# Two groups of heads change places, stack loads are spread over key tiles, and the late output sums move to VectorE

## The chip, the cores and the metric

The kernel runs on one core of one Trainium2 chip. The core has a matrix engine (TensorE, PE in the profile, with its weight loads as PEld), a vector engine (VectorE, DVE), an activation engine (ScalarE, ACT), a general engine (GpSimd, POOL) and a queue engine (SyncE, SP). Transfers (DMAs) are issued from the instruction queues of SP, GpSimd and ScalarE, and 16 DMA engines carry them out. Each engine works through its own instructions in order and waits for others by semaphores.

The metric is the time of the device in microseconds (us) for one execution; of several executions the median counts, less is better.

## The reference: what is computed

One transformer layer over 2048 tokens of width 576, in float32: layer norm, attention with 32 heads of 18 columns each, a residual sum, layer norm again, and a gated feed-forward network of width 4608 with its own residual sum.

```python
qkv = (x @ wqkv).reshape(B, S, 3, H, Dh)          # H = 32 heads, Dh = 18
scores = einsum("bhqd,bhkd->bhqk", q, k) * Dh ** -0.5
o = einsum("bhqk,bhkd->bhqd", softmax(scores), v)
h = x + o.transpose(0, 2, 1, 3).reshape(B, S, D) @ wo   # x was normalised before wqkv
h2 = h + (gelu(hn @ w_gate) * (hn @ w_up)) @ w_down     # hn = layernorm(h)
```

Column f of `o` (0 to 575), and so row f of `wo`, belongs to head f // 18.

## The kernel before, in words

**Numbers in two halves.** Most products are made of float16 numbers, each float32 number cut into a high and a low part, with three products for one. The high and low parts of q and k go to two tensors in device memory, `qk_hi` and `qk_lo` (L343), and come back as *stacks*: for each head 54 rows that hold high, high, low of q against high, low, high of k.

**Groups, blocks, key tiles.** The 32 heads form `NG` = 8 groups of four, and the 2048 queries form `NB` = 4 blocks of 512. The attention loop (L1352) runs over n = 0 to 31 with group g = n // 4 and query block qc = n % 4, and in each n over `kt` = 0 to 15, the key tiles of 128 keys. For one key tile `score` (L702) makes the scores of four heads on TensorE and their exponentials on ScalarE (L723, L725), and `weigh` (L729) multiplies them with V and with a column of ones, whose result is the sum for the softmax. In the same loop `maxima` (L809) makes the row maxima for a query block that comes one and a half n later: scores on TensorE (L645), maxima on VectorE (L659, L657). What an engine does is in the order in which the program writes it out (the kernel switches automatic ordering off for all engines); pieces of side work are written as generators, and `take(it)` puts the next piece at that place of the order.

**Stacks.** There are two sets of stacks. `load_stacks(g)` (L583) writes one set with 24 transfers of 18 rows by 2048 (72 KB each): 12 for the first pair of heads, issued from SP, and 12 for the second, issued from GpSimd. `load_ends(g)` (L612) issues 8 smaller transfers from SP; `key_steps(g)` (L621) makes differences of keys from them on GpSimd, which `maxima` uses. The loop calls both loads for the next group at kt = 10 of the group's first block (L1390; at kt = 2 of the second block in group 0), `key_steps` at kt = 10 and 13 of its second block. For group 0 all this stands ahead of the loop (L1323 to L1325).

**Output of one block.** `out_block(n)` (L744) runs in three pieces during n + 1. First, at kt = 1 (0 from late in n = 30 on), ScalarE and VectorE copy the sums out of PSUM, and a transfer fetches the softmax denominators (L752). At kt = 3 the reciprocals are made (GpSimd up to n = 27, VectorE after that), sent to device memory (L767) and broadcast back to all rows by four transfers from SP (L770). At kt = 9 (6 for the blocks n = 29 and 30) the output is multiplied with them, and cut into a high and a low part (L773 to L779): on GpSimd for n up to 29, on VectorE for n = 30 and 31. Then the rows go by transfers into `XT`, the left operand of the product with `wo` (L783 to L799). `XT` holds the 576 columns of `o` in four chunks of 128 and a last one of 64. A transfer of 18 rows that lies in one of the first four chunks carries both parts (L795); rows of the last chunk need one transfer for the high and one for the low part (L799). Each head has two halves of 256 queries. So the rows of heads 28 to 31 (columns 504 to 575, of which 512 to 575 are in the last chunk) need 18 transfers, those of other groups mostly 8. The queues take turns: SP and GpSimd, for n = 30 ScalarE too, for n = 31 SP, GpSimd, SP, GpSimd, ScalarE.

**Product with wo, and the late part of the loop.** From kt = 9 of n = 30 on the maxima are done, and the loop takes half a tile of the product with `wo` at each key tile instead (step `L` of `LATE`, L1347): `wo_pairs` for the tokens of query blocks 0 and 1 (the tiles 0, 4, 1, 5 and so on), then `wo_block(2)`. One half is 14 matmuls (L325) that read `XT` in the order of its chunks, and one operation of VectorE that adds the residual (L875). Rows that are ready go on to the second layer norm and to the first sums of the feed-forward network (`rows0`, on VectorE, GpSimd and SP's transposes). Beside it GpSimd cuts weights of the feed-forward network from n = 28 on (`split_early`, and the sums of `split_matrix`, L1077). `wo` itself is scaled and cut by `prepare_wo` (L835) during n = 2, with a few VectorE operations on its scales at both ends (L838, L845, L846).

**Ahead of the loop.** Weights of q, k and v come in by `load_w` and `load_chunks` from SP, the v weights in three transfers into `wf[2]` (L498), whose norm ScalarE takes at L180. `v_rows` (L387) puts V's columns into the groups' places by their number.

## Time and profile before

| | |
|---|---|
| time before, median of 3 runs | 2592.74 us (2591.53 to 2593.41) |
| the profiled execution | 2588.55 us, of which 2586.8 us from the first to the last instruction (span) |
| granted clock of TensorE, mean | 0.997 |
| TensorE busy | 2532.3 us (98%) |
| VectorE busy | 1991.4 us (77%) |
| ScalarE busy | 1664.1 us (64%) |
| GpSimd busy | 908.3 us (35%) |
| transfers | 120.99 MB, mean 47 GB/s |

The span has three stretches: q, k and v with the first maxima (to about 205 us), the attention (about 205 to 1376 us, one n in some 35 us until late in n = 30), and the feed-forward network (to the end). In the profile's lines a group of instructions is named by line, engine and operation, with the tiles it writes and reads (`X<-nat` is a transfer of output rows into `XT`, `rc` the reciprocals, `mx` the maxima, `WK` the exponentials, `A` and `W` the two sets of stacks). "Idle before" is the time in which the engine stood still just before an instruction, with what ended it; "issue" there means that the engine waited for nothing that the profile shows.

### The profile page before, as it was taken

What the parts mean: (1) busy time and instruction counts of PE and PEld (TensorE: products, weight loads), DVE (VectorE), ACT (ScalarE), POOL (GpSimd) and SP (SyncE); (2) the same over time, 40 slices, a digit from 0 to 9 for tenths busy, and PEclk for the clock granted to TensorE, in tenths of its full rate; (3) what the DMA queues carried; (4) which work ended last, traced back from release to release, by engine and by line L of the source; (5) the groups of instructions that cost most, each with busy time, mean ns of one, the idle gap of its engine ahead of it and who ended that gap; (6) DMA issues with size and microseconds to landing.
All of it is one profiled execution on the core that took longest, in us unless ns stands there. A gap on an engine that the chain in (4) does not pass through costs nothing.

```text
span 2586.8 us, 96735 instructions
## 1 busy us (share of the span) xinstructions
PE 2532.3 (98%) x41245; PEld 1440.3 (56%) x41245; DVE 1991.4 (77%) x3887; ACT 1664.1 (64%) x2967; POOL 908.3 (35%) x1290
## 2 busy tenths in 40 slices
PE   8999999999999999999989999999999999999999
PEld 4645555555555555555555555555555555555555
DVE  8479999999999999999856674757575756565653
ACT  7438999999999999999845433424242434333332
POOL 4301634432434333346946332323132323232221
PEclk9999999999999999999999999999999999999999
DMA  8621010110101010101234410101010101010110
GB/s 223 159 70 53 19 46 22 26 41 18 47 19 49 21 46 21 44 22 35 57 76 93 85 51 12 53 12 37 28 34 30 35 30 35 30 34 30 34 56 37
DMA packets 177086, 120.99 MB, mean 47 GB/s; under 512 B 93854, under 2 KB 153433, under 8 KB 176653
## 3 DMA queue, kind: packets, MB, share of 16 engines
q1 hardware_dynamic: 162987, 96.18, 14.0%
q0 software_dynamic: 13312, 18.54, 2.8%
q8 instruction: 322, 5.28, 0.9%
q14 instruction: 111, 0.91, 0.1%
q10 hardware_dynamic: 354, 0.08, 0.0%
HBM read 80.05 MB, written 15.01 MB: 37 GB/s over the span
## 4 chain that ended last, share of the span: by engine, by line
PE 74%; DVE 14%; ACT 6%; issue 3%; POOL 2%; DMA 1%; SPq 0%; ACTq 0%; DVEq 0%; POOLq 0%
PE more L1209 14%; PE bank L1209 14%; PE bank L325 10%; DVE mx L659 9%; PE more L325 8%; PE bank L645 6%; PE bank L737 5%; ACT WK L725 4%; PE quad L737 4%; PE quad L325 3%; DVE nat L657 3%; PE pair L714 2%; PE bank L714 2%; PE quad L645 1%; PE pair L325 1%
## 5 line engine op out<-in xcount | busy, mean ns | idle before, releaser
L659 DVE TENSOR_REDUCE mx<-bank 128x1 f32<-128x512 f32 x1064 | 707.4, 683 | 23.4 <-PE bank L645 21.5
L737 PE MATMUL bank<-WK,V 64*32 64x256 f32 x8192 | 636.6, 379 | 8.2 <-ACT nat L748 8.0
L737 PE MATMUL quad<-WK,V 64*32 64x256 f32 x8192 | 639.4, 380 | 0.4 <-issue 0.2
L725 ACT ACTIVATE WK<-bank 128x512 f32<-128x512 f32 x780 | 543.3, 700 | 1.8 <-PE bank L714 1.6
L1209 PEld LDWEIGHTS <-W 128*128 128x128 f16 x2394 | 233.9, 98 | 278.9 <-issue 0.4
L325 PEld LDWEIGHTS <-WK 128*128 128x128 f16 x3456 | 338.0, 98 | 88.6 <-POOL WK L1223 0.3
L725 ACT ACTIVATE WK<-quad 128x512 f32<-128x512 f32 x488 | 345.3, 708 | 0.5 <-PE quad L714 0.3
L659 DVE TENSOR_REDUCE mx<-pair 128x1 f32<-128x512 f32 x488 | 336.8, 690 | 3.9 <-PE pair L645 0.4
L723 ACT ACTIVATE WK<-pair 128x1024 f32<-128x1024 f32 x268 | 293.7, 1096 | 47.1 <-PE pair L714 37.1
L737 PEld LDWEIGHTS quad<-WK,V 64*32 64x32 f32 x8192 | 236.4, 106 | 26.2 <-issue 0.9
L645 PEld LDWEIGHTS <-W 54*32 54x32 f16 x4096 | 140.8, 89 | 179.3 <-issue 116.8
L737 PEld LDWEIGHTS bank<-WK,V 64*32 64x32 f32 x8192 | 216.5, 105 | 34.1 <-ACT nat L748 17.4
L325 PE MATMUL more<-W,WK 128*128 128x288 f16 x1728 | 235.4, 286 | 0.0
L325 PE MATMUL bank<-W,WK 128*128 128x288 f16 x1728 | 235.3, 286 | 0.0
L759 POOL TENSOR_TENSOR rp<-rc,minus_one 128x4 f32<-128x4 f32 x112 | 111.4, 1009 | 340.7 <-DMA rc<-nat 340.7
L645 PEld LDWEIGHTS <-A 54*32 54x32 f16 x4096 | 132.2, 89 | 175.7 <-issue 118.5
L1209 PE MATMUL more<-X,W 128*128 128x512 f16 x792 | 223.9, 379 | 0.0
L645 PE MATMUL bank<-W 54*32 54x512 f16 x2048 | 203.5, 383 | 7.4 <-DVE mx L659 0.9
L645 PE MATMUL bank<-A 54*32 54x512 f16 x2220 | 202.8, 383 | 6.8 <-DVE mx L659 0.4
L1077 POOL TENSOR_TENSOR A<-A 128x384 f32<-128x384 f32 x136 | 137.3, 1030 | 199.4 <-DMA A<-in_B_w_up_dram 99.8
L1209 PE MATMUL more<-V,W 128*128 128x512 f16 x720 | 202.5, 379 | 0.0
L1223 POOL TENSOR_TENSOR WK<-tmp,WK 128x512 f16<-128x512 f32 x73 | 88.7, 1214 | 306.7 <-ACT WK L1220 306.5
(361 smaller groups left out, 5053.5 us busy)
## 6 DMA issues: line engine op xcount, KB each, us to landing
A<-in_B_w_down_dram SPq DMA_DIRECT2D x8, 1152.0 KB
nat<-rc SPq DMA_DIRECT2D x128, 64.0 KB
A<-in_B_w_gate_dram SPq DMA_DIRECT2D x64, 128.0 KB
A<-in_B_w_up_dram SPq DMA_DIRECT2D x64, 128.0 KB
qk_hi<-tmp SPq DMA_DIRECT2D x36, 128.0 KB
qk_lo<-tmp SPq DMA_DIRECT2D x36, 128.0 KB
out_dram<-nat SPq DMA_DIRECT2D x16, 288.0 KB
nat<-in_A_x_dram SPq DMA_DIRECT2D x3, 1152.0 KB
```

The costliest lines, as they stand in the source:

```text
L325: nc.tensor.matmul(dst, a, b, start=(i == 0), stop=(i == len(pairs) - 1))
L645: mm = [nc.tensor.matmul(pm[c : c + CT, :TB], Q[r, q0 + c : q0 + c + CT], keys, start=True, stop=True) for c in range(0, P, CT)]
L657: nc.vector.tensor_tensor_reduce(row, pm[:, :TB], row, 1.0, LOWEST, ALU.add, ALU.max, dst)
L659: red = nc.vector.tensor_reduce(dst, pm[:, :TB], axis=AX.X, op=ALU.max)
L714: mm.append(nc.tensor.matmul(pS[c : c + CT, :TB], K[r, k0 : k0 + CT], Q[r, qc * TB : (qc + 1) * TB], start=True, stop=True))
L723: act = nc.scalar.activation(pe, pair, AF.Exp, scale=ex_reg)
L725: act = nc.scalar.activation(pe[:, heads[0] % 2], bank_at(bank)[:, :TB], AF.Exp, scale=ex_reg)
L737: nc.tensor.matmul(acc[CT * c : CT * c + CT, :QH], Vg[n // NB][ks, v : v + CT], pes[(2 * kt + q) % NPE][ks, j, qh * QH : (qh + 1) * QH], s ...
L759: nc.gpsimd.tensor_tensor(rc[:, c : c + 4], den[:, c : c + 4], minus_one.to_broadcast([P, 4]), op=ALU.pow)
L1077: op(W8[:, d], W8[:, a], W8[:, b])
L1209: nc.tensor.matmul(bank, w, x_, start=start and i == 0, stop=i == len(mm) - 1, skip_group_check=not start)
L1223: nc.gpsimd.tensor_sub(hl[:, 2 * i + j], v, hh[:, 2 * i + j])
```

## The change

The work stays the same; its order, its places and its queues differ.

1. `ORDER` lets the last two groups change places: group 6 of the loop handles heads 28 to 31, group 7 heads 24 to 27. The columns of V's weights are loaded so that these groups find theirs at the usual place: nine transfers of 432, 72 and 72 columns instead of three of 576.
2. `load_stacks` becomes a generator that yields after each pair of transfers (one from SP, one from GpSimd), and `load_group` puts one transfer of `load_ends` behind each of the first eight pairs. From the same place in the loop as before, one such step is taken at each key tile. For group 0 all steps are run at once.
3. In `out_block` VectorE makes the products and cuts of n = 29 too. The rows go out from SP and GpSimd in turn, for n = 29 from SP, SP, GpSimd; ScalarE issues none of them any more.
4. The third piece of `out_block` for n = 29 is taken at kt = 8 of n = 30 instead of 6, that of n = 30 at kt = 5 of n = 31 instead of 6.
5. The scales of `wo` are made ahead of the loop by `scale_wo`; `prepare_wo` only cuts.

```diff
--- before.py
+++ after.py
@@ -347,6 +347,7 @@
 
 
 
+    ORDER = [g for g in range(NG) if g != NG - 2] + [NG - 2]
     G4 = 4 * VC
     VGAP = 768
     VH = NG // 2
@@ -495,7 +496,10 @@
     load_chunks(wf[1], wqkv[:, D:QK], nc.sync, range(2, NK + 1))
     load_x(1)
     qk_tiles(0, 0)
-    load_w(wf[2], wqkv[:, QK:], nc.sync)
+    G72 = 4 * DH
+    for a, b, n_ in ((0, 0, (NG - 2) * G72), ((NG - 2) * G72, (NG - 1) * G72, G72),
+                     ((NG - 1) * G72, (NG - 2) * G72, G72)):
+        load_w(wf[2][:, :, a : a + n_], wqkv[:, QK + b : QK + b + n_], nc.sync)
     take(n1, 4)
     qk_tiles(0, 1)
     take(n1, 1)
@@ -582,18 +586,15 @@
 
     def load_stacks(g):
         st = sets[g % 2]
-        for pr in range(2):
-            eng = nc.sync if pr == 0 else nc.gpsimd
-            Q, K = st[pr]
-            for j in range(2):
-                h = 4 * g + 2 * pr + j
-                o = 64 * j
-                kr = slice(D + h * DH, D + (h + 1) * DH)
-                qr = slice(h * DH, (h + 1) * DH)
-                for i, (qs, ks) in enumerate(((qk_hi, qk_hi), (qk_hi, qk_lo), (qk_lo, qk_hi))):
-                    rows = slice(o + i * DH, o + (i + 1) * DH)
-                    eng.dma_start(Q[rows], qs[qr])
-                    eng.dma_start(K[rows], ks[kr])
+        for j in range(2):
+            o = 64 * j
+            for i, (qs, ks) in enumerate(((qk_hi, qk_hi), (qk_hi, qk_lo), (qk_lo, qk_hi))):
+                rows = slice(o + i * DH, o + (i + 1) * DH)
+                for m, src in ((0, qs), (1, ks)):
+                    for pr, eng in enumerate((nc.sync, nc.gpsimd)):
+                        f = m * D + (4 * ORDER[g] + 2 * pr + j) * DH
+                        eng.dma_start(st[pr][m][rows], src[f : f + DH])
+                    yield
 
     nat1 = nat.rearrange("p t d -> p (t d)")
     HB = NB // 2
@@ -611,12 +612,20 @@
 
     def load_ends(g):
 
-        kr = slice(D + 4 * g * DH, D + (4 * g + 1) * DH)
+        kr = slice(D + 4 * ORDER[g] * DH, D + (4 * ORDER[g] + 1) * DH)
         for e, src in zip(ends, (qk_hi, qk_lo)):
             for s in range(DQ):
                 nc.sync.dma_start(
                     e[s * DH : (s + 1) * DH],
                     src[kr].rearrange("r (k s i) -> r k s i", k=NB, s=DQ)[:, :, s])
+                yield
+
+    def load_group(g):
+
+        it = load_ends(g)
+        for _ in load_stacks(g):
+            take(it)
+            yield
 
     def key_steps(g):
 
@@ -769,7 +778,7 @@
         for c in range(4):
             nc.sync.dma_start(rcb[32 * c : 32 * c + 32], rd_rows[c : c + 1].to_broadcast([32, TB]))
         yield
-        if n < NS - 2:
+        if n < NS - 3:
             nc.gpsimd.tensor_mul(oT, oT, rcb)
             nc.gpsimd.tensor_copy(ohl[:, 0], oT)
             nc.gpsimd.tensor_sub(ohl[:, 1], oT, ohl[:, 0])
@@ -777,11 +786,10 @@
             nc.vector.tensor_mul(oT, oT, rcb)
             (nc.scalar.copy if n == NS - 1 else nc.vector.tensor_copy)(ohl[:, 0], oT)
             nc.vector.tensor_sub(ohl[:, 1], oT, ohl[:, 0])
-        engs = ring([nc.sync, nc.gpsimd] + ([nc.scalar] if n == NS - 2 else
-                                            [nc.sync, nc.gpsimd, nc.scalar] if n == NS - 1 else []))
+        engs = ring([nc.sync, nc.gpsimd] if n != NS - 3 else [nc.sync, nc.sync, nc.gpsimd])
         quads_of = ohl.rearrange("p s (i c) -> i p s c", i=2)
         for hh in range(4):
-            f, end = (4 * g + hh) * DH, (4 * g + hh + 1) * DH
+            f, end = (4 * ORDER[g] + hh) * DH, (4 * ORDER[g] + hh + 1) * DH
             r = 0
             while f < end:
                 c, p = divmod(f, P)
@@ -834,14 +842,20 @@
 
     def prepare_wo():
 
-        e_o = e_wo[0]
-        s_o = pow2(e_o, -1, 268, "s_wo")
+        s_o = scales_o[0]
         for c in range(NK + 1):
             nc.gpsimd.tensor_scalar_mul(of[:, c], of[:, c], s_o)
             yield
             nc.gpsimd.tensor_copy(oh[:, c], of[:, c])
             nc.gpsimd.tensor_sub(ol[:, c], of[:, c], oh[:, c])
             yield
+
+    scales_o = []
+
+    def scale_wo():
+
+        e_o = e_wo[0]
+        scales_o.append(pow2(e_o, -1, 268, "s_wo"))
         nc.vector.tensor_add(e_o, e_o, e_keep)
         nc.vector.tensor_copy(u_o, pow2(e_o, 1, -151, "u_wo"))
 
@@ -1320,8 +1334,7 @@
     qk_tiles(3, 0)
     init_set(sets[0])
     qk_tiles(3, 4, 5)
-    load_stacks(0)
-    load_ends(0)
+    run(load_group(0))
     run(key_steps(0))
     load_w(of, wo, nc.gpsimd)
     sums = chain(norm_wo(), raw_norms())
@@ -1338,6 +1351,7 @@
             take(sums)
         if i == 5 * AHEAD // 4 - 6:
             nc.scalar.activation(root, eps, AF.Exp)
+            scale_wo()
     run(sums)
     m_ring = ring([singles[2], quads[1]])
     accs = (singles[3], quads[2])
@@ -1349,6 +1363,7 @@
     rows_at = {4 * (i + 1) + k: c for i in range(TPB) for k, c in ((1, 2), (3, 3), (4, 3))}
     rows = rows0()
     in_order.enter_context(tc.manual_schedule(engines={EngineType.SP}))
+    loads = iter(())
     for n in range(NS):
         g, qc = divmod(n, NB)
         late = n > NS - NB
@@ -1372,7 +1387,7 @@
                 else:
                     take(side)
             halves += [(n, kt, accs, q) for q in range(2)]
-            if n and kt in (2 if n == NS - 1 else 3, 6 if n > NS - 3 else 9):
+            if n and kt in (2 if n == NS - 1 else 3, {NS - 1: 5, NS - 2: 8}.get(n, 9)):
                 take(ob)
             if n == NS - NB + 1 and 4 <= kt < 9:
                 nc.sync.dma_start(nat[:, kt - 4], xv[:, kt - 4])
@@ -1388,8 +1403,8 @@
                 run(fill)
                 init_set(sets[1])
             if g + 1 < NG and (qc, kt) == ((1, 2) if g == 0 else (0, 10)):
-                load_stacks(g + 1)
-                load_ends(g + 1)
+                loads = load_group(g + 1)
+            take(loads)
             if g + 1 < NG and qc == 1 and kt == 10:
                 steps_made = key_steps(g + 1)
                 take(steps_made)
```

## The prediction, made before the changed kernel was run

> **What bounds the kernel now.** I read the page first, then the table of 65 us windows, then the timelines of single engines where a window falls short. TensorE is the engine to look at: its line on the page, then the windows (per row: length, busy us of PE, PEld, DVE, ACT and POOL, granted clock, DMA share, GB/s).
>
> ```profile
> PE 2532.3 (98%) x41245; PEld 1440.3 (56%) x41245; DVE 1991.4 (77%) x3887; ACT 1664.1 (64%) x2967; POOL 908.3 (35%) x1290
> ```
>
> ```profile
> 325.00:390.00 65.00, 62.78 (x1867) 35.58 (x1864) 63.32 (x120) 63.83 (x120) 23.01 (x41) 1.00 0.16 44
> ...
> 520.00:585.00 65.00, 62.42 (x1856) 34.70 (x1851) 63.43 (x120) 63.61 (x119) 24.84 (x41) 1.00 0.15 36
> 585.00:650.00 65.00, 63.69 (x1908) 35.94 (x1893) 64.34 (x124) 65.00 (x123) 18.16 (x32) 1.00 0.07 17
> 650.00:715.00 65.00, 63.15 (x1904) 35.46 (x1888) 64.31 (x122) 64.61 (x121) 28.63 (x48) 1.00 0.18 46
> ...
> 910.00:975.00 65.00, 63.40 (x1884) 35.28 (x1873) 64.03 (x123) 64.48 (x122) 28.02 (x49) 1.00 0.17 47
> ...
> 1495.00:1560.00 65.00, 65.00 (x388) 37.97 (x387) 48.34 (x100) 27.42 (x39) 20.19 (x19) 1.00 0.14 41
> ```
>
> In the attention ScalarE has no gap at all (65.00 of 65 in the row at 585, as in most), so there every microsecond in which ScalarE idles is lost. After 1376 TensorE is full (65.00 in the last row): what is saved earlier is kept to the end. The big losses lie between, in the last two query blocks, where TensorE sets the pace. TensorE's timeline there (start, length, and in brackets the idle time before and who ended it):
>
> ```profile
> 1287.48 1.28 PE L325 MATMUL bank<-W,X 128*128 128x288 f16 x9
> 1290.54 0.54 PE L325 MATMUL bank<-W,X 128*128 128x288 f16 x3 [1.78 <-DMA X<-nat]
> 1296.00 0.64 PE L325 MATMUL bank<-W,X 128*128 128x288 f16 x2 [4.92 <-DMA X<-nat]
> ...
> 1299.16 1.89 PE L325 MATMUL quad<-W,X 128*128 128x288 f16 x14
> ...
> 1333.02 1.89 PE L325 MATMUL quad<-W,X 128*128 128x288 f16 x14
> ...
> 1336.30 1.89 PE L325 MATMUL bank<-W,X 128*128 128x288 f16 x14
> ...
> 1344.08 0.63 PE L714 MATMUL pair<-W 56*32 56x512 f16 x8 [5.30 <-ACT WK L723]
> ...
> 1346.46 3.54 PE L325 MATMUL quad<-W,X 128*128 128x288 f16 x14
> ...
> 1351.46 0.79 PE L325 MATMUL bank<-W,X 128*128 128x288 f16 x5
> ```
>
> One key tile with its half product of wo takes 1336.30 - 1333.02 = 3.28 us. The first stall stretches one of them to 1299.16 - 1287.48 = 11.68, a loss of 8.40 (6.70 idle, 1.70 slow). The second: 1351.46 - 1336.30 = 15.16 for two, a loss of 8.60 (5.30 idle, 3.30 slow). The slow part is the clock, in windows of the same columns:
>
> ```profile
> 1292.12:1298.95 6.83, 2.95 (x50) 1.19 (x50) 0.52 (x1) 0.73 (x1) 1.44 (x3) 0.50 0.39 110
> ...
> 1343.32:1350.15 6.83, 6.07 (x54) 2.82 (x61) 0.11 (x1) 3.58 (x6) 1.86 (x3) 0.50 0.03 6
> ```
>
> Half clock follows both stalls, so removing a stall removes its slow part too. The Trainium skill ("TensorE: Matmul & The Clock Gate", "Why this matters for your kernels") says that one idle window of some 3 us halves the clock; the trace agrees (5.30 us idle, then 0.50). By its penalty (throttled time times a half) the two windows would cost 6.8 us where the spacing shows 5.0, since TensorE still idles in part of them; the sum would be 1.8 better.
>
> **First stall: the sums of the block before (n = 29).** GpSimd, SP and VectorE:
>
> ```profile
> 1281.38 4.00 POOL L1077 TENSOR_TENSOR A<-A 128x384 f32<-128x384 f32 x4
> 1285.34 1.28 POOL L773 TENSOR_TENSOR nat<-nat 128x512 f32<-128x512 f32 x1
> ```
>
> ```profile
> 1272.41 2.96 SPq L770 DMA_DIRECT2D nat<-rc  x4
> ...
> 1289.36 6.03 SPq L799 DMA_DIRECT2D X<-nat  x8
> ```
>
> ```profile
> 1279.08 0.68 DVE L657 CUSTOM_DVE_ANT_0 nat<-quad,nat 128x512 f32<-128x512 f32 x1
> ```
>
> The broadcast reciprocals are issued by 1275.4, but GpSimd, in order, first cuts weights until 1285.3, sums until 1288.5, and then SP needs to 1295.4 for its half of 18 row transfers (eight of its nine in the row). TensorE gets on at 1296.0. After the change VectorE does the sums at kt = 8, right behind its last maximum, which ends at 1279.8. Their price on VectorE is shown one block later, with ScalarE's share of that block's rows:
>
> ```profile
> 1336.43 0.69 DVE L777 TENSOR_TENSOR nat<-nat 128x512 f32<-128x512 f32 x1
> ...
> 1337.62 0.69 DVE L779 TENSOR_TENSOR nat<-nat 128x512 f16<-128x512 f32 x1
> ```
>
> ```profile
> 1337.62 5.28 ACTq L799 DMA_DIRECT2D X<-nat  x6
> 1343.01 1.02 ACT L723 ACTIVATE WK<-pair 128x1024 f32<-128x1024 f32 x1 [8.46 <-DMA X<-nat]
> ```
>
> 1338.31 - 1336.43 = 1.9, so the sums are ready at 1281.7 instead of 1288.5. The last group now holds heads 24 to 27, output rows 432 to 503, all in one chunk of 128: 8 transfers of 18 rows (L795) instead of 18. Six go to SP, two to GpSimd:
>
> ```profile
> L795 POOL DMA_DIRECT2D X<-nat x128: 520/593/788, 262.7 to 1393.0; - x128
> L795 SPq DMA_DIRECT2D X<-nat x128: 645/786/1381, 263.5 to 1389.3; - x128
> ```
>
> ```profile
> X<-nat POOLq DMA_DIRECT2D x100, 18.0 KB, 1.8
> ```
>
> The sixth of SP starts at 1281.7 + 5 x 0.79 = 1285.6 and lands some 1.8 later (GpSimd's row; SP's landing is not shown): 1287.4. GpSimd's two start when the four additions of L1077 end, 1285.4 at the latest, and land by 1285.4 + 0.6 + 1.8 = 1287.8. Chunk 3 is wanted by the tenth of the 14 products, at 1288.76 (1287.48 + 1.28). That is 1 us of margin: I take the whole 8.40, and keep 0 to 8.40 for the range. Behind the sums on VectorE waits only L875 of kt = 9, whose product is not ready before 1282.8; no maxima are left. If the broadcast landed late VectorE would wait with that L875 behind it, and TensorE two halves later; but it has 1279.8 - 1275.4 = 4.4 us to land.
>
> **Second stall: the rows of n = 30.** ScalarE waits for VectorE's sums, issues six transfers, and only then computes the exponentials (8.46 idle). The change leaves this block to SP and GpSimd, 4 transfers each, 4 x 0.79 = 3.2 us, so ScalarE waits for nothing: 8.60. What is late next is the rows themselves, wanted by the product of block 2 at kt = 9, two key tiles (6.6 us) after 1336.30, so at 1342.9. Issued one key tile earlier than now (kt = 5), at about 1335 behind SP's transposes, they land by 1335 + 3.2 + 1.8 = 1340. Covered. The last block (n = 31) loses ScalarE's transfers too; TensorE has no gap there, so 0.
>
> **Stacks, one pair of transfers a key tile.** The loads of the next group start at kt = 10 of its first block, now 24 stack and 8 end transfers at once. Shortly after, TensorE waits for nothing that the profile shows:
>
> ```profile
> 380.54 0.39 PE L645 MATMUL quad<-W 54*32 54x512 f16 x2 [1.01 <-issue]
> ```
>
> ScalarE's missing time in the windows of such loads is 1.17 + 1.39 + 0.39 + 0.52 = 3.47 us (rows 325, 520, 650, 910), against 0.00 in the row at 585, which has none. I read it as code that comes late behind the burst. Spread, a pair (144 KB) and an end transfer go out every 2.2 us. Bounds: 0 if the cause is another, 3.5 if all goes; I take 3.3. The queues they pass: SP's wait for the reciprocals at kt = 1 to 3 delays the last pairs by a few us, and they are first read at kt = 8 of the third block, over 40 us on. On GpSimd each costs 0.5 us, as now.
>
> **The prelude pays.** SP's transfers, TensorE's first maxima, the read of V's weights, and the load's windows:
>
> ```profile
> 22.42 0.59 SPq L285 DMA_DIRECT2D WK<-in_A_wqkv_dram  x1
> ...
> 99.80 3.63 SPq L617 DMA_DIRECT2D nat<-qk_lo  x4
> ```
>
> ```profile
> 30.25 0.67 ACT L180 ACTIVATE A<-WK 128x576 f16<-128x576 f32 x1
> ```
>
> ```profile
> 102.61 0.77 PE L645 MATMUL bank<-A 54*32 54x512 f16 x16
> ```
>
> ```profile
> 88.00:100.50 12.50, 12.50 (x104) 9.98 (x103) 0.00 (x0) 8.38 (x30) 4.91 (x11) 1.00 0.60 154
> 100.50:105.00 4.50, 4.50 (x48) 3.04 (x46) 1.95 (x4) 2.55 (x10) 0.70 (x2) 1.00 0.20 40
> ```
>
> V's columns come in 9 transfers instead of 3: 6 x 0.59 = 3.5 us more on SP, ending at 23.0 + 3.5 = 26.5, before ScalarE reads them at 30.25. Bounds 0 and 3.5; I take 0.5. In the first load the end transfers now stand among the stacks, so the last stack leaves SP last, by 103.4 (where the ends are now), and the second maximum wants it at 102.7. The transfers themselves end with 0.20 x 4.5 = 0.9 us of work after 100.5, so about 101.4 if nothing idles; bounds 0 and 8.5; I take 0.5.
>
> **Small parts.** The scale of wo moves ahead of the loop. Its four late operations sit on a full VectorE now:
>
> ```profile
> 308.16 0.72 DVE L845 CUSTOM_DVE_ANT_0 e_wo<-e_wo,e_keep 128x2 uint16<-128x2 uint16 x1
> ...
> 309.37 0.69 DVE L659 TENSOR_REDUCE mx<-bank 128x1 f32<-128x512 f32 x1
> ```
>
> From 308.16 to 309.37 is 1.2 us; ahead of the loop VectorE has room. Bounds 0 and 1.2; I take 0.5. Heads 28 to 31 take the 18 row transfers in blocks 24 to 27: 5 more of 0.5 us on GpSimd, busy 28 of 65 there (row 910); 0 while that idle time covers it, 2.5 a block if not.
>
> **Sum.** 8.4 + 8.6 + 3.3 + 0.5 - 0.5 - 0.5 = 19.8 us. The profiled execution took 2588.55 (span 2586.8), 4.2 below the median 2592.74; so 2568.8 for it, and 2592.74 - 19.8 = 2572.9 for the median.
>
> **Rivals.** *The first stall stays in part*: the rows land after 1288.76, because GpSimd's two come late or VectorE waits. For it: 1 us of margin. Against: all inputs are there 4 us early. Up to 8.4 back; with half, 2577. *The gaps after the stack loads stay*: their cause is not the burst. For it: the profile names none, and the loads differ (1.39 against 0.39; three of the seven show next to nothing). 2572.9 + 3.3 = 2576.2. The Trainium skill ("Runtime: NRT & Kernel Launch", "Instruction fetch mechanics") speaks for this one: code is fetched in blocks while the one before executes, "mostly hidden"; by that 2576.2. The stall of 1.01 "issue" speaks against it. *Slower: every pair costs what a burst costs now.* A burst costs 3.47 / 7 = 0.5 us; seven groups with 12 pairs each would make 42 us, so 2572.9 + 3.3 + 42 = 2618. It decides from (2592.74 - 2576.2) / 84 = 0.2 us a pair. Against: the four broadcasts of every block go out as closely and leave ScalarE at 65.00:
>
> ```profile
> 397.51 1.71 SPq L770 DMA_DIRECT2D nat<-rc  x4
> ```
>
> **Chances.** Forecast 0.72, first stall in part 0.12, gaps stay 0.11, slower 0.05. No change can be told within 0.2% (5.2 us): faster 0.94, same 0.02, slower 0.04. Range: at the low end the whole of every gain without the prelude's cost (8.4 + 8.6 + 3.5 + 1.2 = 21.7, so 2571), less the runs' spread and gaps not listed, 2565; at the high end the first stall's whole 8.4 back, 2581.3, with the spread 2583.
>
> **What would show it.** No idle time of TensorE over 1 us at L325 or L714 in the last two blocks, clock 1.00 there, key tiles 3.28 us apart; sums of n = 29 on VectorE about 1.9 us right behind the last maximum; no transfer in ScalarE's queue there; ScalarE at 65.00 in the windows with loads; no new gap of TensorE before its first maxima. A TensorE gap before `X` in the last blocks, or ScalarE's gaps at group changes unchanged, would prove the matching part wrong.

## The result, and the profile after

| | before | after |
|---|---|---|
| median (6 runs each) | 2589.65 us (2584.45 to 2593.41) | 2570.51 us (2569.81 to 2573.94) |
| ratio, 95% interval | | 0.993 (0.9916 to 0.9944) |
| profiled execution, span | 2588.55, 2586.8 us | 2570.03, 2568.2 us |
| TensorE's granted clock, mean | 0.997 | 1.0 |

The prediction used the first three of the six runs of before (2592.74). The changed kernel is 19.1 us faster by the medians, 18.5 us by the profiled executions; 19.8 was predicted. Lines of the changed kernel stand some ten further down: L654 and L668 are the maxima (L645, L659 before), L732 the exponentials (L723), L746 and L757 the product with V and the copy of its sums (L737, L748), L786 to L788 VectorE's sums (L777 to L779), L803 the row transfers (L795), L889 the residual (L875), L1091 the cut of weights (L1077).

TensorE's line on the page of the changed kernel, against 2532.3 us before; TensorE does the same matmuls:

```profile
PE 2526.9 (98%) x41245; PEld 1439.5 (56%) x41245; DVE 1992.3 (78%) x3890; ACT 1664.1 (65%) x2967; POOL 908.0 (35%) x1290
```

The waits of TensorE in the changed kernel from 1262 to 1359 us (the last two query blocks), all of them (us in total, times, longest), and its timeline there:

```profile
PE bank L746 <- ACT nat L757: 0.3, 1, 0.3
```

```profile
1283.43 1.89 PE L325 MATMUL quad<-W,X 128*128 128x288 f16 x14
1286.71 1.89 PE L325 MATMUL bank<-W,X 128*128 128x288 f16 x14
1289.99 1.89 PE L325 MATMUL quad<-W,X 128*128 128x288 f16 x14
...
1333.70 1.89 PE L325 MATMUL bank<-W,X 128*128 128x288 f16 x14
1336.98 1.89 PE L325 MATMUL quad<-W,X 128*128 128x288 f16 x14
1340.26 1.89 PE L325 MATMUL bank<-W,X 128*128 128x288 f16 x14
```

Both stalls are gone in this execution: half a tile of the product with `wo` every 3.28 us, in both places. The sums and row transfers of n = 29 (first stall), on VectorE, SP and GpSimd:

```profile
1278.73 1.03 DVE L786 TENSOR_TENSOR nat<-nat 128x512 f32<-128x512 f32 x1
1279.85 1.06 DVE L787 CAST nat<-nat 128x512 f16<-128x512 f32 x1
1280.94 1.37 DVE L788 TENSOR_TENSOR nat<-nat 128x512 f16<-128x512 f32 x1
1282.24 0.51 DVE L889 SCALAR_TENSOR_TENSOR nat<-bank,u_o,nat 128x288 f32<-128x288 f32 x1
```

```profile
1282.34 4.92 SPq L803 DMA_DIRECT2D X<-nat  x6
```

```profile
1277.13 4.64 POOL L1091 TENSOR_TENSOR A<-A 128x384 f32<-128x384 f32 x4
1282.61 1.24 POOL L803 DMA_DIRECT2D X<-nat  x2 [0.84 <-DVE nat L788]
```

The sums stand right behind the last maximum, as predicted, but take 3.6 us (1278.73 to 1282.31), not 1.9.

The 65 us windows of the changed kernel (same columns as before):

```profile
325.00:390.00 65.00, 63.63 (x1900) 35.68 (x1892) 64.29 (x122) 64.93 (x122) 24.13 (x44) 1.00 0.16 41
520.00:585.00 65.00, 63.83 (x1912) 36.04 (x1897) 64.62 (x124) 65.00 (x122) 26.42 (x44) 1.00 0.14 36
...
650.00:715.00 65.00, 63.84 (x1912) 36.03 (x1904) 64.50 (x122) 65.00 (x122) 27.70 (x47) 1.00 0.19 49
910.00:975.00 65.00, 63.75 (x1912) 35.80 (x1890) 64.17 (x122) 64.83 (x121) 31.50 (x54) 1.00 0.19 48
```

ScalarE's missing time in these four was 3.47 us before and is 0.24 now.

To see where the gain lies, the two profiled executions are laid beside each other at points that both have: the start of the first maxima, of the first scores, of ScalarE's copy of block n's sums (L748 before, L757 after), and of the feed-forward network's first matmuls. A difference that grows between two points was lost between them:

```
start after - start before, us
first maxima   +0.66      n = 3    +1.52      n = 30      -9.16
first scores   +2.06      n = 24   -1.91      n = 31     -17.81
n = 1          +2.02      n = 29   -0.77      feed-fwd.  -17.76
n = 2          +1.58                          end        -18.54
```

So: ahead of the first scores 2.06 lost, scales of `wo` 0.44 gained (n = 1 to 2), stack loads 3.43 (n = 3 to 24), then 1.14 lost (n = 24 to 29), first stall 8.39, second 8.65, and 0.78 gained in the feed-forward network.

### The profile page after: what moved, and what is told of

Its sections match the earlier page's. It is cut to its first block, busy times and chain, and to the rows that moved or that the text cites. A ratio compares the mean times of both kernels' runs of the same rounds, so it can differ in the third digit from the quotient of the medians.

```text
span 2568.2 us, 96735 instructions
## 1 busy us (share of the span) xinstructions
PE 2526.9 (98%) x41245; PEld 1439.5 (56%) x41245; DVE 1992.3 (78%) x3890; ACT 1664.1 (65%) x2967; POOL 908.0 (35%) x1290
## 4 chain that ended last, share of the span: by engine, by line
PE 75%; DVE 13%; ACT 6%; issue 3%; DMA 1%; SPq 0%; POOL 0%; ACTq 0%; DVEq 0%; POOLq 0%
PE bank L1223 15%; PE more L1223 15%; PE bank L325 10%; DVE mx L668 9%; PE more L325 8%; PE bank L654 6%; PE bank L746 5%; ACT WK L734 5%; PE quad L746 4%; PE quad L325 3%; DVE nat L666 3%; PE pair L723 2%; PE bank L723 2%; PE quad L654 1%; PE quad L723 1%
## 5 line engine op out<-in xcount | busy, mean ns | idle before, releaser
L668 DVE TENSOR_REDUCE mx<-bank 128x1 f32<-128x512 f32 x1064 | 707.8, 683 | 25.0 <-PE bank L654 23.1
L746 PE MATMUL bank<-WK,V 64*32 64x256 f32 x8192 | 634.5, 379 | 8.0 <-ACT nat L757 7.9
L746 PE MATMUL quad<-WK,V 64*32 64x256 f32 x8192 | 637.2, 379 | 0.6 <-issue 0.4
L668 DVE TENSOR_REDUCE mx<-pair 128x1 f32<-128x512 f32 x488 | 336.8, 690 | 3.9 <-PE pair L654 0.5
L732 ACT ACTIVATE WK<-pair 128x1024 f32<-128x1024 f32 x268 | 293.5, 1095 | 28.6 <-PE pair L723 26.3
L746 PEld LDWEIGHTS quad<-WK,V 64*32 64x32 f32 x8192 | 235.7, 105 | 25.1 <-issue 0.7
L654 PEld LDWEIGHTS <-W 54*32 54x32 f16 x4096 | 140.5, 89 | 181.2 <-issue 119.1
L746 PEld LDWEIGHTS bank<-WK,V 64*32 64x32 f32 x8192 | 216.0, 105 | 32.9 <-ACT nat L757 17.4
L654 PEld LDWEIGHTS <-A 54*32 54x32 f16 x4096 | 132.4, 89 | 176.2 <-issue 118.6
L654 PE MATMUL bank<-W 54*32 54x512 f16 x2048 | 203.6, 383 | 7.1
L654 PE MATMUL bank<-A 54*32 54x512 f16 x2220 | 203.1, 383 | 7.5 <-DMA A<-qk_hi 0.9
L1091 POOL TENSOR_TENSOR A<-A 128x384 f32<-128x384 f32 x136 | 137.6, 1033 | 196.1 <-DMA A<-in_B_w_up_dram 97.7
```

What stands on the lines that cost most here:

```text
L654: mm = [nc.tensor.matmul(pm[c : c + CT, :TB], Q[r, q0 + c : q0 + c + CT], keys, start=True, stop=True) for c in range(0, P, CT)]
L668: red = nc.vector.tensor_reduce(dst, pm[:, :TB], axis=AX.X, op=ALU.max)
L732: act = nc.scalar.activation(pe, pair, AF.Exp, scale=ex_reg)
L746: nc.tensor.matmul(acc[CT * c : CT * c + CT, :QH], Vg[n // NB][ks, v : v + CT], pes[(2 * kt + q) % NPE][ks, j, qh * QH : (qh + 1) * QH], s ...
L1091: op(W8[:, d], W8[:, a], W8[:, b])
```

## Experiments

Single profiled executions are compared at the same points. Each figure is the change against the kernel before over that stretch; a minus is a gain. "After, again" is a second profiled execution of the changed kernel; the last three kernels come in the section on the first scores:

```
kernel (us, profiled execution)   first     n=3 to   n=24 to  n=29 to  n=30 to
                                  scores    n=24     n=29     n=30     n=31
after            2570.03          +2.06    -3.43    +1.14    -8.39    -8.65
after, again     2569.49          +1.99    -3.42    +0.65    -8.00    -8.65
late part alone  2580.30          +0.72    +1.10    +1.15    -3.12    -7.68
no exchange      2576.48          +2.31    -4.15    +0.23    -2.98    -8.31
sums on GpSimd   2573.35          +3.49    -3.44    +0.78    -6.02    -8.61
ScalarE's queue  2576.45          +2.16    -3.44    +1.40    -8.40    -3.68
sums at kt = 9   2575.60          +6.25    -3.43    +0.69    -6.23    -8.65
all at once      2575.46          +3.40    +0.17    +1.32    -8.11    -8.65
two a key tile   2569.58          +1.98    -3.44    +0.65    -7.93    -8.65
burst at kt = 15 2590.30          +0.05    -0.19    +0.71    +0.15    +0.24
new order, gr. 0 2591.51          +1.48    -1.08    +0.99    +0.03    -1.16
old order, gr. 0 2570.21          +3.14    -3.44    +0.64    -8.40    -8.65
and V in 3, cut  2568.77          +2.16    -4.02    -0.14    -8.40    -8.65
```

### The first stall: three ways to bring it back

**The late part alone** (the kernel before, with VectorE's sums, the two queues and the key tiles of the change; places, loads and scales as before).

```diff
-        if n < NS - 2:
+        if n < NS - 3:
-        engs = ring([nc.sync, nc.gpsimd] + ([nc.scalar] if n == NS - 2 else ...
+        engs = ring([nc.sync, nc.gpsimd] if n != NS - 3 else [nc.sync, nc.sync, nc.gpsimd])
-            if n and kt in (2 if n == NS - 1 else 3, 6 if n > NS - 3 else 9):
+            if n and kt in (2 if n == NS - 1 else 3, {NS - 1: 5, NS - 2: 8}.get(n, 9)):
```

> The kernel before with the late part of the change alone: sums of n = 29 on VectorE, their rows to SP and GpSimd, the key tiles 8 and 5; no change of places, so the last heads' block still makes 18 row transfers, and the loads stay at once. Theory A (the sums' lateness and the count of transfers both made the first stall): SP's 12 of 18 leave from about 1282.3 on at 0.7 to 0.8 us each, the last lands near 1292.5 to 1293.5, some 4 us after TensorE wants it; the first stall stays at 4 to 6 us with its slow clock, the second is gone: about 11 to 13 us off the profiled execution before (2576 to 2578). Theory B (the sums' place alone decides, the change of places of the groups is not needed): both stalls gone, 17 us off (2571.5). If the second stall is still there, 0 to 4 us off.

**No exchange of places** (the changed kernel, with heads and V in the old order).

```diff
-    ORDER = [g for g in range(NG) if g != NG - 2] + [NG - 2]
+    ORDER = list(range(NG))
...
+    load_w(wf[2], wqkv[:, QK:], nc.sync)
```

> The changed kernel with the heads in their old order and V loaded in 3 transfers; all else of the change stays. Theory A: the first stall comes back in part, 4 to 6 us with its slow clock, since 18 transfers leave in the last group's block; the way to the first scores gets 0.5 to 0.8 us shorter (V in 3 transfers, of the 2.06 us that the changed kernel lost there); the 1.1 us that the changed kernel lost in blocks 24 to 29 come back if the 18 transfers that moved into blocks 24 to 27 were their cause, and stay if not. Against the changed kernel +2 to +5 us. Theory B (the change of places does nothing): 0.6 us less than the changed kernel.

**The sums of n = 29 on GpSimd** (the changed kernel; 8 transfers stay).

```diff
-        if n < NS - 3:
+        if n < NS - 2:
```

> The changed kernel with the sums of n = 29 back on GpSimd, where they stand behind its four additions that cut weights; their 8 row transfers stay. Theory A (the sums' lateness made the first stall): the sums end near 1288.5 to 1290 instead of 1282.3, the last rows land near 1295, TensorE waits 4 to 6 us and then has the half clock for a window: 6 to 8 us more than the changed kernel (2574 to 2576 for the profiled execution). Theory B (18 transfers instead of 8 made it): 8 transfers need 4 us and TensorE waits under 1 us: 0 to 1 us more.

The row transfers of SP in the kernel without the exchange and TensorE behind them; then the same two in the kernel with GpSimd's sums:

```profile
1282.08 1.51 SPq L800 DMA_DIRECT2D X<-nat  x2
1283.63 7.55 SPq L804 DMA_DIRECT2D X<-nat  x10
```

```profile
1286.40 1.65 PE L325 MATMUL bank<-W,X 128*128 128x288 f16 x12
1291.67 0.40 PE L325 MATMUL bank<-W,X 128*128 128x288 f16 x2 [3.63 <-DMA X<-nat]
```

```profile
1285.84 4.92 SPq L803 DMA_DIRECT2D X<-nat  x6
```

```profile
1287.77 1.28 PE L325 MATMUL bank<-W,X 128*128 128x288 f16 x9
1291.27 0.77 PE L325 MATMUL bank<-W,X 128*128 128x288 f16 x5 [2.22 <-DMA X<-nat]
```

In each TensorE gets on 0.5 us after SP's last issue ends (1291.18, 1290.76). Both causes are real. Of the 8.39 us, early sums alone bring 3.0 to 3.1 (two kernels; with 18 transfers TensorE still idles 3.6 us, then a half clock), 8 transfers alone bring 6.0 (2.22 us idle, full clock), both together all. Theory A holds for the kernels with 18 transfers. For GpSimd's sums its 6 to 8 us were too much: the loss is 2.4, since the half clock did not come. The exchange of places carries the larger part. How the eight transfers are divided between the queues (six to SP, two to GpSimd) was not varied by itself.

The totals of the two kernels with 18 transfers miss what was expected. The late part alone is 8.25 us ahead of the kernel before instead of 11 to 13: at the second stall TensorE still waits 0.8 us (0.5 for rows, 0.3 for VectorE), and 0.72, 1.10 and 1.15 are lost elsewhere (table). The kernel without the exchange is 6.5 us behind the changed one instead of 2 to 5, of which 1.5 go to a window of half clock after the first scores (last section); its first scores come no earlier (+2.31), though V has 3 transfers there.

**Sums one key tile later** (kt = 9) measures the margin.

```diff
-            if n and kt in (2 if n == NS - 1 else 3, {NS - 1: 5, NS - 2: 8}.get(n, 9)):
+            if n and kt in (2 if n == NS - 1 else 3, {NS - 1: 5}.get(n, 9)):
```

> The changed kernel with the sums of n = 29 and their rows one key tile later, at 9 instead of 8 (3.28 us, and behind one more operation of VectorE). Theory A (the margin is 0.7 to 1 us): TensorE waits for the rows 2 to 3 us, without a window of half clock or with a short one: 2 to 4 us more than the changed kernel. Theory B (the rows are wanted later than I read it, the margin is over 3 us): 0.

```profile
1288.19 4.92 SPq L803 DMA_DIRECT2D X<-nat  x6
```

```profile
1290.44 1.28 PE L325 MATMUL bank<-W,X 128*128 128x288 f16 x9
1293.72 0.77 PE L325 MATMUL bank<-W,X 128*128 128x288 f16 x5 [2.00 <-DMA X<-nat]
```

At kt = 9 GpSimd's additions are over before the sums begin, and each is as short as the prediction had it:

```profile
1281.30 4.00 POOL L1091 TENSOR_TENSOR A<-A 128x384 f32<-128x384 f32 x4
```

```profile
1286.24 0.68 DVE L786 TENSOR_TENSOR nat<-nat 128x512 f32<-128x512 f32 x1
1287.01 0.43 DVE L787 CAST nat<-nat 128x512 f16<-128x512 f32 x1
1287.48 0.69 DVE L788 TENSOR_TENSOR nat<-nat 128x512 f16<-128x512 f32 x1
```

So the same sums take 1.9 us apart from these additions and 3.6 beside them, and the additions 4.00 and 4.64.

Lost: 2.16 us, as theory A said (most of what its total has beside that lies ahead of the first scores, below). TensorE got on 0.6 us after SP's last issue ended (1293.11). In the changed kernel SP's last issue ends at 1287.26 and chunk 3 is wanted at 1286.71 + 1.28 = 1287.99, so by 0.5 to 0.6 us its margin is 0.1 to 0.2 us. It just fits, and not in each execution: in the second one of the changed kernel VectorE's first product took 1.50 us instead of 1.03, and TensorE waited for the rows (0.31 us with two steps a key tile):

```profile
1286.16 1.28 PE L325 MATMUL bank<-W,X 128*128 128x288 f16 x9
1287.68 0.77 PE L325 MATMUL bank<-W,X 128*128 128x288 f16 x5 [0.24 <-DMA X<-nat]
```

### The second stall: ScalarE's queue

```diff
-        engs = ring([nc.sync, nc.gpsimd] if n != NS - 3 else [nc.sync, nc.sync, nc.gpsimd])
+        engs = ring([nc.sync, nc.sync, nc.gpsimd] if n == NS - 3 else
+                    [nc.sync, nc.gpsimd] + ([nc.scalar] if n == NS - 2 else []))
```

> The changed kernel with ScalarE back in the ring for the rows of n = 30 (2 or 3 of the 8 transfers); the sums stay on VectorE at key tile 5. Theory A (ScalarE's wait for the sums is what cost the second stall): ScalarE stands 2 to 4 us at its first transfer, and 2 x 0.75 us go on issuing; as TensorE has about 1 to 2 us of work ahead there, it loses 2 to 4 us; with under 3 us idle the clock stays full. Theory B (the six issues alone cost it, not the wait): 2 x 0.75 us in ScalarE, hidden: 0 us. Theory C (any use of ScalarE's queue costs the whole second stall): 8.6 us.

ScalarE and TensorE of that kernel, then the 3.41 us behind the wait (columns as in the windows):

```profile
1327.15 2.28 ACTq L804 DMA_DIRECT2D X<-nat  x2
1329.55 1.02 ACT L732 ACTIVATE WK<-pair 128x1024 f32<-128x1024 f32 x1 [5.79 <-DVE nat L890]
```

```profile
1330.62 0.41 PE L723 MATMUL pair<-W 56*32 56x512 f16 x8 [2.64 <-ACT WK L732]
```

```profile
1331.17:1334.58 3.41, 3.41 (x31) 1.50 (x31) 0.00 (x0) 2.28 (x4) 3.23 (x5) 0.50 0.52 120
```

5.0 of the 8.65 us are back (8.65 - 3.68). ScalarE waits for VectorE's sums, issues two transfers, and TensorE runs dry for 2.64 us. That is theory A, and more than its 2 to 4: the expectation left out the half clock, which came here after under 3 us of idle time.

### The loads of the stacks

**All at once in the changed kernel (24 stack transfers, then 8 end transfers, for group 0 too); two steps a key tile; and, in the kernel before, the burst at kt = 15 instead of 10.**

```diff
-                loads = load_group(g + 1)
+                load_at_once(g + 1)
```

> The changed kernel with all loads of stacks and ends issued at once again, as before the change, group 0's in the old order too. Theory A (the burst makes the gaps of ScalarE after group changes): ScalarE's gaps of 0.4 to 1.4 us a load come back, 3.4 us from the fourth block to the 25th; of the 2.06 us that the changed kernel lost ahead of the first scores 0.9 to 1.4 come back, since the last stack leaves SP earlier: in all 2 to 2.5 us more than the changed kernel. Theory B (the gaps have another cause, and went for another reason): no gaps, 0.9 to 1.4 us less than the changed kernel.

```diff
-            take(loads)
+            take(loads, 2)
```

> The changed kernel with two steps of the loads a key tile instead of one (four stack transfers and two end transfers every 2.2 us, over 6 key tiles). Theory A (a rate at which code still comes in time is what counts): 0 to 0.5 us more than the changed kernel between the fourth block and the 25th. Theory B (each transfer costs something wherever it stands): 0, since their number is the same. Theory C (how many stand close together is all that counts): about half of the 3.4 us return, 1.7 us more.

```diff
-            if g + 1 < NG and (qc, kt) == ((1, 2) if g == 0 else (0, 10)):
+            if g + 1 < NG and (qc, kt) == ((1, 2) if g == 0 else (0, 15)):
```

> The kernel before with one figure changed: the loads of the next group, all at once, start at key tile 15 of a group's first block instead of key tile 10 (group 1's as before). Theory A (the burst makes the gaps): the gaps of TensorE and ScalarE behind the loads of groups 2 to 7 come about 5 x 2.2 = 11 us later and have the same sum, 3 us or so; group 1's stays where it is. Theory B (the place in the code makes them, not the transfers): they stay where they were.

With the loads at once the whole gain of 3.43 us is gone (n = 3 to 24: 0.17 lost instead), as theory A said. TensorE's gap behind one of these loads, and ScalarE's:

```profile
529.20 0.39 PE L735 MATMUL pair<-A 56*32 56x512 f16 x3 [1.25 <-issue]
```

```profile
529.70 1.02 ACT L744 ACTIVATE WK<-pair 128x1024 f32<-128x1024 f32 x1 [1.41 <-PE quad L666]
```

The records of the transfers suggest what TensorE waits for. Queue q8 ("instruction") brings the program in blocks; on the changed kernel's page it has

```profile
q8 instruction: 322, 5.28, 0.9%
```

322 blocks of 16 KB. In the attention of the kernel before one starts every 4.31 us (median). Behind a burst the next one comes late, and ScalarE's gap follows some 9 us after the start of the block before it (two of the 14 gaps here, all that these kernels have from 340 to 1175 us, come 13 to 14 us after it, the second one of the second row and that of the third):

```
kernel               start of a block, us to the next   ScalarE's gap behind it, us
before                371.5  6.6                        1.07
                      512.6  6.3                        0.73 + 0.66
                      654.2  5.9                        0.39
                      939.6  5.9                        0.52
all at once           378.4  6.8                        0.98
                      519.8  6.9                        1.41
                      800.9  6.8                        0.63
                      942.2  5.8                        0.16
                     1082.9  6.2                        0.42
late part alone       376.8  6.7                        1.44
                      517.8  7.9                        2.00
                      660.0  7.4                        1.50
                     1082.1  6.2                        0.63
after, two a tile     none over 5.4 from 340 to 1175    none from 340 to 1175
```

The run shows that the burst brings the gaps, and the records that code is late just there, by and large the later the longer the gap; that the one works through the other is read from their coming together. Not every late block costs: one of 5.9 us in the kernel with all loads at once has no gap behind it, nor have blocks of 5.6 and 5.9 us in two kernels with spread loads (sums on GpSimd at 522.7, old order for group 0 at 802.2). The Trainium skill ("Runtime: NRT & Kernel Launch", "Instruction fetch mechanics") calls the cost of crossing from one block to the next "mostly hidden". The trace agrees up to 5 us or so between blocks; from 5.4 to 5.9 us some cost nothing and others up to 0.9 us (burst at kt = 15, the block at 799.3), and all beyond 6 us cost 0.4 to 2.0.

Two steps a tile cost nothing (n = 3 to 24: -3.44 and -3.43): theories A and B. Theory C's 1.7 us did not come, but the run tests it only in part, and the reason shows in the queues: the prediction's "a pair every 2.2 us" isn't what runs. SP and GpSimd have nothing to wait for at those key tiles and go ahead in order. SP in the changed kernel, at one load:

```profile
515.18 0.44 SPq L596 DMA_DIRECT2D W<-qk_hi  x1
515.67 0.85 SPq L618 DMA_DIRECT2D nat<-qk_hi  x1
516.58 0.47 SPq L596 DMA_DIRECT2D W<-qk_hi  x1
517.09 0.80 SPq L618 DMA_DIRECT2D nat<-qk_hi  x1
```

GpSimd sends nine of its twelve within 5 us (512.38 to 516.98). What stretches the load is the end transfer between SP's stack transfers: 1.4 us a pair instead of 0.35, and this is so with two steps a tile too. That edit moved only the ends of the two queues (GpSimd's last three from 535.5 to 516.8 us, SP's last from 539.8 to 528.5). GpSimd's twelve then leave within 6 us, as closely as in a burst, and cost nothing; SP's first eight still leave some 1.4 us apart. For the same reason the burst at kt = 15 told nothing. It was issued at the same times (GpSimd's first at 512.4 in both kernels), and left ScalarE's gap behind this load where it was (521.25 against 521.18). The edit moved no transfer, so it speaks for neither theory.

### Ahead of the first scores

**The kernel before with group 0's loads in the new order alone** (2591.51 us; 12 pairs of stack transfers, an end transfer after each of the first 8):

```diff
-    load_stacks(0)
-    load_ends(0)
+    load_mixed(0)
```

> The kernel before with one thing of the change: the loads of group 0 in the new order (after each of the first eight pairs of stack transfers an end transfer from SP). V in 3 transfers, all other loads at once, the late part as before. Theory A (in this order SP's last stack leaves and lands later, and TensorE's first maxima wait for it): stack packets end near 103.7 us in place of 101.3 to 102.1, TensorE waits 0.9 to 1.5 us behind its first four maxima, the first scores start 1.5 to 2 us later than in the kernel before. Theory B (the order costs nothing; what is late in the changed kernel comes from its other parts): stacks land by 102.2, no wait, the first scores within 0.8 us of the kernel before, as with the two kernels that kept its first loads.

TensorE of the changed kernel at its first maxima, then of this one:

```profile
103.26 0.40 PE L654 MATMUL bank<-A 54*32 54x512 f16 x4
104.55 0.87 PE L654 MATMUL bank<-A 54*32 54x512 f16 x12 [0.89 <-DMA A<-qk_hi]
```

```profile
102.86 0.40 PE L663 MATMUL bank<-A 54*32 54x512 f16 x4
104.01 0.84 PE L663 MATMUL bank<-A 54*32 54x512 f16 x12 [0.75 <-DVE mx L677]
```

SP's last stack packet ends at 103.68 (changed kernel) and 102.90 (this one), against 101.67 in the kernel before; TensorE's wait of 0.75 is put down to VectorE's first reduction, but the kernel before doesn't wait for that here, and the last packet ended 1.1 us before TensorE went on (0.9 in the changed kernel); I read it as the transfer. The first scores are 1.48 us later, 1.2 of them from the first maxima on: theory A, with figures a little under its own.

The changed kernel was then timed beside one with the old order for group 0 alone, and one that also loads V in 3 transfers and lets V's columns change places when they are cut (its three transfers are not shown):

```diff
-    run(load_group(0))
+    load_at_once(0)
...
-    split_cols(wf[2][:, :, HALF:], s_v, *wv[1])
+    for a, b, n_ in ((0, 0, 2 * G72), (2 * G72, 3 * G72, G72), (3 * G72, 2 * G72, G72)):
+        split_cols(wf[2][:, :, HALF + b : HALF + b + n_], s_v, *(w[:, :, a : a + n_] for w in wv[1]))
```

> The changed kernel itself, timed beside the two that follow: 2570.5 us, 0.993 of the kernel before.

> The changed kernel with the loads of group 0 alone in the old order (stacks first, then the ends); V still in 9 transfers. Theory A (the last stack of group 0 comes late): the 0.89 us gap of TensorE ahead of its first maxima goes, the first scores start 0.9 to 1.4 us earlier than in the changed kernel, and this is kept to the end: 2569.1 to 2569.6. Theory B (the 9 transfers of V alone made the loss, or it is swallowed later): 0.

> As the kernel with group 0's loads in the old order, and V loaded in 3 transfers again; its columns change places when ScalarE and the others cut them into halves of precision (three operations per part instead of one). Theory A (the prelude's loss is the 6 transfers of V and the late stack, 2.06 us in all): 1.5 to 2 us less than the changed kernel, 2568.5 to 2569. Theory B (the smaller cuts cost as much as the transfers): the same as the kernel with 9 transfers and group 0's loads in the old order. If the rest of the 2.06 us is the changed place of something else, 0.9 to 1.4 us less than the changed kernel.

```
                     median, range of 5 runs              ratio to before, 95%         first maxima, first scores
after                2569.49 (2568.80 to 2572.10)         0.9935 (0.9922 to 0.9949)    +0.94, +1.99
old order, group 0   2569.99 (2569.11 to 2571.38)         0.9935 (0.9922 to 0.9949)    +0.99, +3.14
and V in 3, cut      2567.12 (2565.81 to 2568.77)         0.9923 (0.9909 to 0.9936)    +0.58, +2.16
```

The old order gave nothing back. Its stack packets ended at 104.94 us, with 285 ns a packet; in the kernel with V in 3 transfers at 103.77 (278 ns), in the one with all loads at once at 105.33 (277 ns). In the three kernels with the whole stretch of before they took 245 to 252 ns and ended at 101.27 to 102.14. So the new order makes the stacks late in the one kernel, and in the others the old order is late too, by packets that take a tenth longer; why, no run tells. V in 3 transfers is the fastest kernel here: each of its five runs was below each of the changed kernel's, 2.4 us by the medians. Its profiled execution, the slowest of its five, shows 0.7 against the changed kernel's second one: from n = 3 to n = 29 it is 1.4 us ahead (table: 0.60 and 0.79), and it loses 1.5 to a window of half clock after the first scores. Why these blocks run shorter stays open.

## Why the prediction was right, and where not

The time (2570.51, predicted 2572.9, range 2565 to 2583) and the sign are right, and so are the two largest terms: the rows were late, and ScalarE's queue held up its exponentials.

- **First stall, 8.4: 8.39.** Right in this execution, and partly by luck. The step "their price on VectorE is shown one block later", 1.9 us, failed: beside GpSimd's additions the sums took 3.6 us, and those additions 4.64 instead of 4.00; apart from them (kt = 9) they took 1.9. Another error of the other sign helped: rows landing "some 1.8 later", a figure of GpSimd's, were there 1.3 to 1.4 us after the start of SP's last issue (0.8 to issue, 0.5 to 0.6 behind it). In the second execution 0.24 us of waiting came back and the term was 8.00, so the rival that the stall stays in part came true by that much. "Half of 18 transfers" was the larger cause, GpSimd's lateness the smaller.
- **Second stall, 8.6: 8.65.** Right. TensorE has no wait there.
- **Stacks, 3.3: 3.43,** 3.42 to 3.44 in each of seven executions with spread loads and V in 9 transfers. That the burst makes the gaps is shown; the reading "code that comes late behind the burst" is supported by the blocks of q8, but no run changed the blocks alone. The picture of one pair every 2.2 us is wrong; the rival priced at 42 us ("every pair costs what a burst costs") and the one that leaves the gaps both fell.
- **Scales of `wo`, 0.5: 0.44.** Right.
- **The prelude, -0.5 - 0.5: -2.06.** Mis-sized, in both terms. For V's 9 transfers the step "ending at 26.5" failed: the ninth left only at 29.29, since SP waited 3.0 us before it for an earlier transfer of weights to land, and ScalarE's read waited (SP's issues, the wait of SP, ScalarE):

```profile
25.64 0.61 SPq L284 DMA_DIRECT2D WK<-in_A_wqkv_dram  x1
29.29 0.47 SPq L285 DMA_DIRECT2D WK<-in_A_wqkv_dram  x1
```

```profile
SPq L285 <- DMA WK<-in_A_wqkv_dram: 3.0, 1, 3.0
```

```profile
30.89 0.69 ACT L180 ACTIVATE A<-WK 128x576 f16<-128x576 f32 x1 [0.44 <-DMA WK<-in_A_wqkv_dram]
```

  The first maxima started 0.66 later here. The size varies: with two steps a key tile, the same program up to there, SP waited 1.7 us, ScalarE not at all, and they started 0.01 later; the late part alone, with V's 3 transfers, was 0.84 later. For the last stack the step "about 101.4 if nothing idles" failed: it landed at 103.7, and 1.4 more were lost. What the prediction named as proof against it, a gap ahead of the first maxima, is there.
- **Not foreseen: -1.14 in n = 25 to 29.** The moved row transfers of heads 28 to 31 were costed at 0; the runs leave this open. Of the 1.14, 0.53 to 0.54 are lost between n = 24 and n = 27, and so in seven of the eight executions with both the exchange and V in 9 transfers (the eighth, all loads at once, has a burst there and loses 1.05). The kernel without the exchange loses 0.00 there, which speaks for the moved transfers; the one with the exchange and V in 3 loses only 0.06, so they don't cost it by themselves. The rest, n = 27 to 29, varies between executions: 0.61 here and 0.11 in the second one of the same program. The +0.78 in the feed-forward network was not followed up.

## What to carry to other kernels

Before taking the price of an operation from elsewhere in the trace, look at what the other engines do beside it in the new place; a margin of 1 us can be gone by that alone (here the sums took 1.7 us more). A queue that has nothing to wait for runs ahead of the loop: spreading issues in the program spreads them on the chip only if something between them takes time in that queue. Gaps that the profile puts down to nothing ("issue") can be checked against the times at which blocks of code arrive.

## What was not expected of the hardware

**Half clock without a long stall.** TensorE's clock changes on a grid of 3.41 us, whose place differs from execution to execution (from one change to the next the traces have 3.41, 6.83, 44.37, 194.56 or 1280.00 us and the like, all multiples of it). Beside each window of that grid stands TensorE's busy time in it, and whether the clock was halved in the next (worked out from the trace):

```
kernel            window from   busy of 3.41 us   next window
late part alone   1292.5        0.24              half
ScalarE's queue   1327.8        0.70              half
sums at kt = 9     104.8        1.09              half
no exchange       1289.8        1.51              half
no exchange       1286.4        1.69              full
burst at kt = 15  1337.8        1.74              full
sums on GpSimd    1286.9        2.18              full
sums at kt = 9    1292.6        2.33              full
```

In these stretches the clock is halved where TensorE was busy for at most 1.5 us of a window, whatever the length of the stall. The stalls of 2.00 and 2.22 us fell across two windows and cost only themselves; that of 2.64 us lay in one. In all 14 profiled executions, up to their last 10 us, no window with at most 1.51 us is followed by full clock, and none with 1.69 or more by half clock, but for the four of the next paragraph. The Trainium skill ("TensorE: Matmul & The Clock Gate", "Why this matters for your kernels" and "What's actually happening") puts the danger at gaps of over some 3 us, one idle window, and says that the window runs freely. The trace agrees with the second; for the first 1.9 us of idle time in one window were enough.

Another place shows that the grid's place counts. After the first scores TensorE's matmuls are small and it idles 0.85 us; in 4 of 14 profiled executions (no exchange, ScalarE's queue, V in 3 transfers, new order for group 0) a window of half clock follows at 207 to 208 us and costs 1.3 to 1.5 us by the copy of n = 0. In these four an edge of the grid lies 3.2 to 3.8 us behind the first scores, in the other ten it doesn't. Busy time alone (2.56 us in either case) doesn't tell them apart.

**Transfers of the same bytes vary.** In the execution with the sums at kt = 9, whose program is the changed kernel's up to n = 29, the first stacks ended at 106.11 instead of 103.68 us, and TensorE waited 2.37 us for them and then ran a window at half clock. Its first scores came 4.2 us later than the changed kernel's, 1.1 of them lost before the first maxima.
